# Dummy products from the first cleared columns on, sinks' values off VectorE, a later bias and new orders in a fused attention and MLP-Mixer kernel

## The chip, the cores and the metric

The kernel runs on one core of one Trainium2 chip. The metric is the device time of one launch in microseconds (us), taken as the median of several runs. Beside it stands one profiled execution, with its own time, its span and its trace.

## The reference

Attention with 4 sink keys and a sliding window of 128 runs over 4 batches, 8 heads, 768 positions and 64 dimensions; its output is the input of an MLP-Mixer block (token mixing over positions, then channel mixing). All inputs and the output are float32.

```python
scores = scale * np.matmul(q, k.transpose(0, 1, 3, 2))
keep = is_sink | in_window            # sink: key < 4; window: 0 <= query - key < 128
a = softmax(np.where(keep, scores, -1e9))
x = np.matmul(a, v)                   # 4 x 8 x 768 x 64, then heads side by side: 4 x 768 x 512
h = np.maximum(x.transpose(0, 2, 1) @ w_tok1, 0.0) @ w_tok2     # 768 -> 256 -> 768 over positions
u = x + h.transpose(0, 2, 1)
out = u + np.maximum(u @ w_ch1, 0.0) @ w_ch2                    # 512 -> 1536 -> 512 over channels
```

## The kernel before

The 32 heads are worked on as 16 pairs of heads (pair p = 4 b + n, four pairs a batch b). Work for TensorE is cut into 386 **units** of some tenths of a microsecond. The string `ORDERED` lists them in the order in which TensorE runs them; a letter names the kind, a number the unit, "o1-2" means o1 and o2:

- first batch (pairs 0 to 3): `t` turns q (even numbers) or k (odd numbers) of one pair, 64 columns at a time, into PSUM; `m` writes the additive mask of one group of keys into a score bank (pairs 0 to 2); `s` adds the scores of a group (three groups g = 0 to 2 a pair; s10 is the sinks' scores of pairs 2 and 3); `o0` is the sinks' scores of pairs 0 and 1, `o1` to `o8` are the products with the values, two a pair; `g` and `h` are token mixing of the left and of the right half of the channels (g0, g1, h0, h1 the first product, g2 to g4 and h2 to h4 the second, the rest turnings).
- later batches: `w` turns q and k or u, `a` scores (three units a pair, a0 is pair 4), `n` sinks' scores, `v` products with values (two a pair), `k` token mixing.
- channel mixing of all batches: `c` the first product, `x` and `y` the second. From batch 1 on the first product, and for all batches the second, are done in seven instead of eight block products.

Everything that is not TensorE's work (evictions from PSUM, casts, exponentials, loads, stores) is an `Op` with a cost on each engine that may do it. A planner, run when the kernel is built, keeps a clock for each engine, walks through `ORDERED` and places each pending op on the engine where it ends first by these costs; it thereby fixes the program order on ScalarE (ACT), VectorE (DVE), GpSimd (POOL) and SP. Due times written by hand stand for things the planner can't compute: `landed(7700.0)` is the time at which the sinks' value rows are taken to be in SBUF. A constant `BIAS` of 400 ns is added to VectorE's end time when engines are compared.

Loads of the first batch's q and k (`raws`) are plain float32 transfers issued by SP, and are cast to bf16 by an engine (`cast`; pair 3's by GpSimd or VectorE). All other loads are issued by GpSimd and cast in flight. Their order is `LOADS`: v0 is issued first, then `LOADS` names q, k, v of a pair, `t1`, `t2` the weights of token mixing, `c` and `d` blocks of the weights of channel mixing. At most about seven are outstanding, on eight lanes. From pair 8 on q and k are turned by a transposing DMA that SP issues.

At the start, before any data is there, VectorE clears some tiles, and TensorE multiplies a cleared tile of ones by itself seven times, with 512 columns each, by `keep_warm`. The scores have two double banks of PSUM (`sc`), everything else four single ones.

The code that the diff touches:

Of the kernel before, what the change touches and what calls it, by code (L numbers as in the profile page):

```python
# [17 lines left out]
def kernel(  # L18
# [13 lines left out]
    nc = tc.nc  # L32
    B, H, S, D = q.shape
    P = 128
# [11 lines left out]


    ORDERED = (
# [14 lines left out]
    )  # L63
    LOADS = (
        "q4 v1 k4 t1 v2 t2 v3 q5 k5 c2 q6 v4 k6 c3 c0 c1 k7 q7 v5 d3 d0 d2 k9 v6 k8 v7 d1 q8 v8 q9 k10 q12 v9 "
        "q10 k12 k11 q11 v10 k13 v11 v13 q13 k14 q15 q14 v12 k15 v14 v15 "
    )
    ORDER = (1, 2, 7, 6, 4, 5, 3)
    NQ = 6
# [21 lines left out]
    NSC, NMX = 2, 4  # L91
# [7 lines left out]
    def bank(tag, *shape, dtype=FP32, slot=None):  # L99

        n = given[tag].pop(0) if slot is None else slot
        if tag == "sc":
            return sc[n]
        size = 1
        for x in shape:
            size *= x
        flat = all_banks[:, n]
        flat = (flat if dtype == FP32 else flat.bitcast(dtype))[:, 0:size]
        names = "abc"[:len(shape)]
        return flat.rearrange(  # L110
            f"p ({' '.join(names)}) -> p {' '.join(names)}", **{x: v for x, v in zip(names, shape)},
        )

    in_order = tc.keep_in_program_order
    count = [0]

    def issue(x):
        count[0] += 1
        in_order(x)
# [67 lines left out]
    def mm(*args, **kwargs):  # L187
        issue(nc.tensor.matmul(*args, skip_group_check=True, **kwargs))  # L188
# [4 lines left out]
    def copy(e, out, in_):  # L193
        if e == "ACT":
            in_order(nc.scalar.activation(out, in_, AF.Copy))  # L195
        else:
            in_order({"DVE": nc.vector, "POOL": nc.gpsimd}[e].tensor_copy(out=out, in_=in_))
# [16 lines left out]
    NKB = 3  # L214
    kTb = [singles.tile([P, S], BF16, name=f"kT{n}") for n in range(NKB)]
    ones = kTb[NKB - 1][:, 0:4 * P]
    v_sink_f = t_pool.tile([P, 4, HS * 2], BF16, name="uT_sums").rearrange("p n x -> p (n x)").bitcast(FP32)
    v_sink_f = v_sink_f[:, 0:NHP * 2 * D1].rearrange("p (n i d) -> p n i d", n=NHP, i=2)
    in_order(nc.vector.memset(v_sink_f, 0.0))
    in_order(nc.vector.memset(ones, 1.0))  # L220
    settled = singles.tile([1, 2], BF16)
    in_order(nc.gpsimd.memset(settled, 0.0))
    in_order(nc.scalar.activation(settled[:, 1:2], settled[:, 0:1], AF.Copy))

    def keep_warm(n, slot):
        ps = bank("mx", 4 * P, slot=slot)
        for _ in range(n):
            mm(ps, ones[:, 0:P], ones, start=True, stop=True)

    keep_warm(7, 2 * NSC)  # L230

# [30 lines left out]
    v_sink0 = singles.tile([P, NHP, 2, D1], BF16, name="v_sink")  # L262
# [40 lines left out]
    BLOCK = 1.4  # L303
    RECEIPT = 2100.0
    BIAS = 400.0
    FETCH, FETCH_ALONE = 7200.0, 4600.0


# [16 lines left out]
    def landed(at):  # L325
        op = Op({}, None)
        op.done = at
        return op

    class Plan:  # L330
# [57 lines left out]
        def other(self):  # L388
            best = None
            queue = False  # L390
            for n, op in enumerate(self.pending):

                if op.loads:
                    if queue:
                        continue
                    queue = True
                r = self.ready(op)
                if r is not None and op.loads and len(self.landings) + op.loads > LANES:
                    r = max(r, self.landings[len(self.landings) + op.loads - LANES - 1])
                if r is None:  # L400
                    continue
                at = {
                    e: max([self.free[e], r] + [x[1] for x in op.reads if x[0] != e]) for e in op.cost
                }
                e = min(op.cost, key=lambda e: at[e] + op.cost[e] + BIAS * (e == "DVE"))
                t = at[e]
                if best is None or t < best[0] - 1e-6 or (
                    t < best[0] + 1e-6 and e == best[2] and op.urgent > self.pending[best[1]].urgent
                ):
                    best = (t, n, e)  # L410
            return best
# [1013 lines left out]
        return Op({"POOL": 760.0}, lambda e: fn(), lag=1850.0, loads=1)  # L1425

    plan = Plan()
    plan.free.update(PE=4000.0, ACT=3200.0, DVE=3900.0, POOL=5300.0)
    plan.queue = 12800.0
    plan.landings.append(13500.0)  # L1430

    def queue(key, op):
        done[key] = op
        plan.pending.append(op)
# [9 lines left out]
    def cast(p, n, at):  # L1444
        cost = {"POOL": 765.0, "DVE": 475.0} if p == NHP - 1 else {"DVE": 475.0} if p or n else {"ACT": 750.0}
        return Op(cost, lambda e: copy(e, bf_tile(p, n), raws[p][n]), [landed(at)])

    for p, at in enumerate(((4000.0, 5100.0), (6800.0, 8050.0), (9300.0, 10700.0), (12600.0, 14800.0))):
        for n, name in enumerate(("q_bf", "k_bf")):
            queue((name, p), cast(p, n, at[n]))  # L1450
    v_sink = Op({"POOL": 650.0, "DVE": 345.0, "ACT": 500.0}, lambda e: copy(e, v_sink0, v_sink_f), [landed(7700.0)])
    for n in range(NHP):
        done["vs", n] = v_sink
    plan.pending.append(v_sink)
# [144 lines left out]
```

## Time and profile before

| | |
|---|---|
| median of 3 runs | 192.47 us (192.25 to 193.26) |
| profiled execution, its own time | 191.41 us |
| its span in the trace | 189.7 us |
| matmuls | 2269 |
| TensorE, VectorE, ScalarE, GpSimd busy | 181.5, 160.8, 112.1, 78.5 us |
| HBM read, written | 26.75 MB, 6.29 MB |

In the profile, PE is TensorE's matmuls, PEld its weight loads, DVE VectorE, ACT ScalarE, POOL GpSimd, SP SyncE; SPq and POOLq are issues of DMAs. L188 is line 188 of the kernel, the helper that records every matmul; lines L159, L163 and L191 are turnings. In a timeline a row gives start, length, engine, line, operation, output and input tiles, shapes, and the count of instructions merged into it; in brackets stands the idle time of that engine before it and what ended it. TensorE's lengths overlap, since a product's end is modelled with the time that its last column needs to leave the array.

### The profile page before, as it was taken

To read this page: it belongs to the slowest core of one execution; us is meant where nothing else is said; L and a number is where in the kernel's file an instruction comes from. 1 tells how busy PE (TensorE), PEld (TensorE's weight loads), DVE (VectorE), ACT (ScalarE), POOL (GpSimd) and SP (SyncE) were. 2 spreads that over 40 slices of the span, in tenths; PEclk is the share of its full clock that TensorE was granted. 3 is DMA by queue.
4 is the path that set the end of the run, shared out by engine and by line. 5 is a ranking of instruction groups with operands and counts; after the bars stand their busy time and mean duration, and the time that the engine had idled before them with its cause. 6 is when DMAs were issued, how large, how long until landed. Compare 5 with 4: busy or idle time off the path is not lost.

```text
span 189.7 us, 5560 instructions
## 1 busy us (share of the span) xinstructions
PE 181.5 (96%) x2269; PEld 131.7 (69%) x2269; DVE 160.8 (85%) x343; ACT 112.1 (59%) x210; POOL 78.5 (41%) x122
## 2 busy tenths in 40 slices
PE   5889989999999999999999999999999999999992
PEld 1335758766777888766666788865578887668882
DVE  4766969997699999988999998879998968799882
ACT  4698978999974653858875711488842203773000
POOL 5938566374807989472804970150240000000000
PEclk9999999999999999999999999999999999999999
DMA  5999999999999999999999995431100145200035
GB/s 186 288 276 185 188 193 199 200 197 178 175 141 119 168 117 158 135 149 170 292 119 147 166 117 117 180 146 28 28 5 0 28 86 221 111 0 3 0 138 194
DMA packets 82600, 26.31 MB, mean 139 GB/s; under 512 B 70032, under 2 KB 80272, under 8 KB 82576
## 3 DMA queue, kind: packets, MB, share of 16 engines
q0 software_dynamic: 56864, 11.80, 82.8%
q1 hardware_dynamic: 25088, 13.64, 33.0%
q10 hardware_dynamic: 624, 0.53, 0.8%
q8 instruction: 17, 0.28, 0.6%
q14 instruction: 7, 0.06, 0.2%
HBM read 26.75 MB, written 6.29 MB: 174 GB/s over the span
## 4 chain that ended last, share of the span: by engine, by line
PE 87%; DMA 5%; ACT 2%; DVE 1%; issue 1%; POOL 1%; POOLq 0%
PE ps L188 85%; DMA v_aug<-in_v_dram 5%; ACT pT L692 2%; PE ps L191 1%; PE ps L163 1%; DVE x_sb L781 1%; PE ps L597 1%; ACT kT L195 0%; POOL mask_add L247 0%; POOL mask_add L251 0%; DVE pT L711 0%; DVE o_sb L1276 0%; ACT u_sb L195 0%; DVE recip L778 0%; POOL ident L244 0%
## 5 line engine op out<-in xcount | busy, mean ns | idle before, releaser
L692 ACT ACTIVATE pT<-ps 128x1024 bf16<-128x1024 f32 (+1 forms) x48 | 44.9, 963 | 20.1 <-PE ps L188 19.8
L195 ACT ACTIVATE parts<-ps 128x384 f32<-128x384 f32 x54 | 24.6, 490 | 18.0 <-PE ps L188 16.5
L188 PE MATMUL ps<-uT,w_ch 128*128 128x384 bf16 x168 | 33.7, 326 | 0.0
L1164 DVE CUSTOM_DVE_ANT_0 v1T<-ps,parts 128x384 bf16<-128x384 f32 x54 | 28.1, 552 | 6.4 <-PE ps L188 6.0
L188 PEld LDWEIGHTS <-v1T 128*128 128x128 bf16 x288 | 27.6, 98 | 4.4 <-issue 0.2
L188 PEld LDWEIGHTS <-w_ch 128*128 128x128 bf16 x204 | 19.1, 98 | 10.7
L201 ACT ACTIVATE v1T<-ps 128x384 bf16<-128x384 f32 x41 | 19.8, 497 | 9.4 <-PE ps L188 8.8
L188 PE MATMUL ps<-uT_sums,k_f 128*128 128x384 bf16 x108 | 23.5, 326 | 0.0
L188 PEld LDWEIGHTS <-v_sums 128*128 128x128 bf16 x216 | 20.8, 98 | 3.4 <-issue 0.2
L703 POOL TENSOR_SCALAR_AFFINE_SELECT pT<-pT 128x256 bf16<-128x256 bf16 (+1 forms) x20 | 11.6, 612 | 24.4 <-issue 14.6
L188 PEld LDWEIGHTS <-w_tok 128*128 128x128 bf16 x192 | 18.1, 98 | 4.3 <-issue 1.3
L1276 DVE TENSOR_TENSOR o_sb<-ps,u_sb 128x512 f32<-128x512 f32 (+1 forms) x32 | 17.3, 551 | 3.2 <-PE ps L188 3.2
L188 PEld LDWEIGHTS <-k_f 128*128 128x128 bf16 x144 | 13.6, 98 | 8.3 <-issue 0.6
L188 PE MATMUL ps<-q_f,v1T 128*128 128x256 bf16 x144 | 19.0, 273 | 0.0
L188 PE MATMUL ps<-w_ch,v1T 128*128 128x256 bf16 x144 | 18.8, 273 | 0.0
L188 PE MATMUL ps<-q_f,v_sums 128*128 128x256 bf16 x144 | 18.7, 273 | 0.0
L188 PE MATMUL ps<-v_aug,pT 128*128 128x65 bf16 x352 | 17.7, 194 | 1.0 <-DMA v_aug<-in_v_dram 1.0
L188 PEld LDWEIGHTS <-pT 128*128 128x128 bf16 x352 | 16.2, 98 | 3.0 <-DMA v_aug<-in_v_dram 1.5
L181 POOL DMA_DIRECT2D v_aug<-in_v_dram x16 | 16.5, 1037 | 3.2 <-PE ps L188 1.5
L781 DVE TENSOR_TENSOR x_sb<-ps,recip 128x384 bf16<-128x384 f32 x32 | 17.2, 550 | 0.4
L188 PEld LDWEIGHTS <-kT 64*64 64x64 bf16 (+2 forms) x343 | 7.9, 104 | 13.0 <-issue 9.0
L188 PE MATMUL ps<-qT,kT 64*64 64x192 bf16 (+2 forms) x336 | 15.5, 249 | 0.3 <-ACT pT L692 0.3
(91 smaller groups left out, 301.4 us busy)
## 6 DMA issues: line engine op xcount, KB each, us to landing
v_aug<-in_v_dram POOLq DMA_DIRECT2D x16, 192.0 KB, 10.3
w_ch<-in_moe_w_ch_dram POOLq DMA_DIRECT2D x8, 384.0 KB, 10.9
out_dram<-o_sb SPq DMA_DIRECT2D x6, 512.0 KB, 2.9
out_dram<-o_sb SPq DMA_DIRECT2D x10, 256.0 KB, 2.2
q_f<-in_q_dram SPq DMA_DIRECT2D x4, 384.0 KB, 5.1
k_f<-in_k_dram SPq DMA_DIRECT2D x4, 384.0 KB, 5.8
k_bf<-in_k_dram POOLq DMA_DIRECT2D x16, 96.0 KB, 7.6
q_bf<-in_q_dram POOLq DMA_DIRECT2D x16, 96.0 KB, 10.5
```

The source lines that it names most:

```text
L163: issue(nc.tensor.transpose(outs[x][ds(D * h, D), j], t[rows, h, j], ident[rows, rows]))
L181: in_order(nc.gpsimd.dma_start(out=v_aug.rearrange("p i t d -> p (i t) d")[:, :, 0:D], in_=v[b].rearrange("h s d -> (h s) d")[2 * hp * S:2 ...
L188: issue(nc.tensor.matmul(*args, skip_group_check=True, **kwargs))
L191: issue(nc.tensor.transpose(out, in_, ident))
L195: in_order(nc.scalar.activation(out, in_, AF.Copy))
L201: in_order(nc.scalar.activation(out, in_, AF.Relu))
L597: issue(nc.tensor.transpose(outs[x][columns], rows_by_columns[rows, columns], ident[rows, rows]))
L692: in_order(nc.scalar.activation(part(tiles["pT", p][:, :, ds(2 * g, 2)]), of_keys(tiles["ps_s", p, g])[:, :, 0:width(g)], AF.Exp, scale=scale,
L703: in_order(nc.gpsimd.affine_select(out=pt, in_=pt, compare_op=ALU.is_ge, fill=0.0, base=-n, pattern=[[0, nk], [1 - 2 * n, P]], channel_mul ...
L781: in_order(nc.vector.tensor_tensor(out=x_sb[b][:, ts(half, QH), ts(hp, 2 * D)].rearrange("p t (i d) -> p t i d", i=2), in0=tiles["ps_o", p ...
L1164: in_order(nc.vector._custom_dve(TENSOR_ADD_SAT, out=v1_of(i, half), in0=ps, in1=kept[:, n], s0=HUGE, s1=0.0,))
L1276: in_order(nc.vector.tensor_tensor(out=sb(*out), in0=tiles["ps_out", b, t0, key[0]], in1=in1(), op=ALU.add,))
```

## The change

Four things change.

1. The tile of ones is cleared in two steps: its first 128 columns ahead of the other clearings, the rest behind them. `keep_warm` multiplies twelve times with 128 columns and six times with 512, where it did seven times with 512. The planner's clock for TensorE begins at 4900 ns in place of 4000.
2. The conversion of the sinks' values to bf16 may be placed on GpSimd or ScalarE, no longer on VectorE, and its due time is 8500 ns in place of 7700.
3. `BIAS` counts against VectorE only where its start would be later than 25000 ns (`LEAN_FROM`).
4. `ORDERED` and `LOADS` are other permutations of the same units and loads.

```diff
-        "t0-1 m0-1 s0-1 t2 m2 s2 t3 m3 s3 o0 m4 s4 t4 m5 t5 s5 o1-2 m6 s6 w0 m7 s7 t6 m8 t7 s8 o3-4 s9-10 w1 "
-        "s11-12 g0-1 o5-6 g2 a0 o7-8 a1 g3 w2 a2 h0-1 g4-5 h2-4 n0 a3-4 h5 g6 v0 h6 g7 h7 v1 w3 a5 c5 c3 c0 c8 "
-        "c16 c22 c6 c2 a6-7 w4 c14 c13 v2-3 c1 c19 c23 a8-9 n1 k0 c10 c12 c7 k1-2 a10-11 v4-5 k3 c11 c17 c15 v6 "
-        "c21 c4 c9 v7 x0-1 c20 c18 y0 x2 k4 w5 a12 x6 k5 x3 x7 a13-14 x4 y3 x5 x10 n2 k6 y2 v8 x8 k7 a15 y4 x11 "
...
+        "t0 m0 t1 s0 m1 t2 s1 t3 m2 s2 m3 o0 s3 m4 s4 t4-5 m5 t6 s5 o1-2 m6 s6 w0 m7 t7 s7 m8 o3 s8 o4 s9-10 w1 "
+        "s11-12 g0 o5 g1 a0-1 o6-8 g2-4 w2 a2 h0-1 g5-6 n0 h2-5 a3-4 h6 g7 v0-1 h7 c1 c0 c11 c4 c8 w3 a5 w4 c7 "
+        "v2 c10 c2 c9 v3 n1 a6-7 c6 c13 k0 c20 a8 c3 k1 c12 a9-10 k2 v4-5 c16-17 c14 c5 a11 c15 c19 v6 c21 k3 "
+        "c23 x0 c22 v7 a12-13 x1 c18 w5 x2 x6 k4 x3 y0 k5 x4-5 k6 y3 a14 x7 n2 a15-16 y5 v8 x10 k7 y2 x8-9 x11 "
...
-        "q4 v1 k4 t1 v2 t2 v3 q5 k5 c2 q6 v4 k6 c3 c0 c1 k7 q7 v5 d3 d0 d2 k9 v6 k8 v7 d1 q8 v8 q9 k10 q12 v9 "
-        "q10 k12 k11 q11 v10 k13 v11 v13 q13 k14 q15 q14 v12 k15 v14 v15 "
+        "q4 v1 k4 t1 v2 v3 t2 q5 k5 q6 c2 v4 c0 v5 k6 q7 k7 c3 c1 d3 v6 q8 d2 k8 v7 d0 k9 d1 q9 v10 v8 k12 "
+        "q10 k10 v9 k11 q11 q12 q15 v11 k13 q13 k14 q14 v12 k15 v13 v14 v15 "
...
     ones = kTb[NKB - 1][:, 0:4 * P]
+    in_order(nc.vector.memset(ones[:, 0:P], 1.0))
...
     in_order(nc.vector.memset(v_sink_f, 0.0))
-    in_order(nc.vector.memset(ones, 1.0))
+    in_order(nc.vector.memset(ones[:, P:], 1.0))
...
-    def keep_warm(n, slot):
-        ps = bank("mx", 4 * P, slot=slot)
+    def keep_warm(n, width):
+        ps = bank("mx", width, slot=2 * NSC)
         for _ in range(n):
-            mm(ps, ones[:, 0:P], ones, start=True, stop=True)
-
-    keep_warm(7, 2 * NSC)
+            mm(ps, ones[:, 0:P], ones[:, 0:width], start=True, stop=True)
+
+    keep_warm(12, P)
+    keep_warm(6, 4 * P)
...
+    LEAN_FROM = 25000.0
...
-                e = min(op.cost, key=lambda e: at[e] + op.cost[e] + BIAS * (e == "DVE"))
+                e = min(op.cost, key=lambda e: at[e] + op.cost[e] + BIAS * (e == "DVE" and at[e] > LEAN_FROM))
...
-    plan.free.update(PE=4000.0, ACT=3200.0, DVE=3900.0, POOL=5300.0)
+    plan.free.update(PE=4900.0, ACT=3200.0, DVE=3900.0, POOL=5300.0)
...
-    v_sink = Op({"POOL": 650.0, "DVE": 345.0, "ACT": 500.0}, lambda e: copy(e, v_sink0, v_sink_f), [landed(7700.0)])
+    v_sink = Op({"POOL": 650.0, "ACT": 500.0}, lambda e: copy(e, v_sink0, v_sink_f), [landed(8500.0)])
```

20 rows, old and new, of the table ORDERED are left out of this document.

## The prediction, made before the changed kernel ran

> **What bounds the kernel now.** I read the page's share of busy time first, then the stages, then the chain in order of time, and last the rows of single engines in the first 30 us. The page gives the span, the engines and the chain by engine:
>
> ```profile
> span 189.7 us, 5560 instructions
> PE 181.5 (96%) x2269; PEld 131.7 (69%) x2269; DVE 160.8 (85%) x343; ACT 112.1 (59%) x210; POOL 78.5 (41%) x122
> ...
> PE 87%; DMA 5%; ACT 2%; DVE 1%; issue 1%; POOL 1%; POOLq 0%
> ```
>
> TensorE is the bound, but 96% is a mean over stages. The table by stages, TensorE alone (stage, its length, busy us, matmuls, granted clock, DMA share, GB/s), says where the other 4% lie:
>
> ```profile
> 28.40:60.00 31.60, 31.55 (x466) 1.00 1.72 175
> 60.00:120.00 60.00, 60.00 (x790) 1.00 1.91 154
> 120.00:186.40 66.40, 66.35 (x594) 1.00 0.22 72
> ```
>
> From 28.4 us on TensorE waits 0.1 us in 158. The change leaves the products as they are, and in both orders the array's tiling changes 86 times between units (counted from the two lists), so this part can only stay as it is or get worse. What can be won lies ahead of 28.4. The chain in order of time (start, length, what):
>
> ```profile
> 4.17 10.29 DMA v_aug<-in_v_dram
> ...
> 14.50 1.83 PE ps L188 x32
> ...
> 75.36 111.01 PE ps L188 x1090
> ```
>
> Ahead of 14.50 the end is set by one load, the values of pair 0, issued at 4.17 and landed at 14.46. Between 14.50 and 28.45 the rows of TensorE's timeline (start, length, form, count, idle before) show the waits:
>
> ```profile
> 17.34 0.34 PE L159 MATMUL ps<-ident,q_bf 64*128 64x64 bf16 x12
> 17.61 0.50 PE L188 MATMUL ps<-mask_add,ident 128*128 128x384 bf16 x2
> ...
> 18.23 0.33 PE L188 MATMUL ps<-qT,kT 64*128 64x256 bf16 x4
> 18.49 0.36 PE L188 MATMUL ps<-v_aug,pT 128*128 128x65 bf16 x6
> ...
> 19.50 0.39 PE L188 MATMUL ps<-qT,kT 64*128 64x256 bf16 x4
> 19.82 0.40 PE L188 MATMUL ps<-qT,kTs 64*32 64x512 bf16 x4
> ...
> 20.47 0.39 PE L188 MATMUL ps<-qT,kT 64*128 64x256 bf16 x4
> 21.19 0.34 PE L188 MATMUL ps<-qT,kT 64*128 64x256 bf16 x4 [0.33 <-ACT pT L692]
> 21.46 1.48 PE L188 MATMUL ps<-x_sb,w_tok 128*128 128x256 bf16 x12
> 22.79 0.35 PE L188 MATMUL ps<-v_aug,pT 128*128 128x65 bf16 x6
> ...
> 24.52 0.38 PE L188 MATMUL ps<-qT,kT 64*64 64x256 bf16 x8
> 25.41 0.36 PE L188 MATMUL ps<-v_aug,pT 128*128 128x65 bf16 x6 [0.51 <-DMA v_aug<-in_v_dram]
> ...
> 26.42 0.36 PE L188 MATMUL ps<-qT,kT 64*64 64x192 bf16 x8
> 26.71 0.28 PE L188 MATMUL ps<-x_sb,ident 128*128 128x256 bf16 x1
> ...
> 27.87 0.31 PE L188 MATMUL ps<-qT,kT 64*64 64x192 bf16 x8
> 28.45 1.47 PE L188 MATMUL ps<-x_sb,w_tok 128*128 128x256 bf16 x12 [0.27 <-DVE x_sb L781]
> ```
>
> By the order list these are t6 at 17.34, s8 at 18.23, o3 at 18.49, s9, s10 and s11 from 19.50, s12 at 21.19, g0 and g1 at 21.46, o5 at 22.79, a0 at 24.52, o7 at 25.41, a1 at 26.42, g3 at 26.71, a2 at 27.87, h0 at 28.45. Three waits: s12 for ScalarE to empty a score bank, o7 for the values of pair 3, h0 for VectorE. I price each from start to next start, since the idle column leaves out the modelled tail of the product before. s11 to s12 is 0.72 where s9 to s10 is 0.32: 0.40 lost. a0 to o7 is 0.89 where a1 to g3, as many products, is 0.29: 0.60 lost. a2 to h0 is 0.58 against 0.29: 0.29 lost. Together 1.29 us.
>
> The landings that pace this stretch can be read on GpSimd, which waits for a lane of its load queue (timeline, GpSimd), and from what the queries on v_aug give as least, median and longest time from issue to landing:
>
> ```profile
> 8.74 1.02 POOL L181 DMA_DIRECT2D v_aug<-in_v_dram  x1
> ...
> 13.66 0.82 POOL L197 CAST q_bf<-q_f 128x768 bf16<-128x768 f32 x1 [3.19 <-DMA q_f<-in_q_dram]
> ...
> 18.55 0.75 POOL L206 DMA_DIRECT2D w_ch<-in_moe_w_ch_dram  x1 [0.91 <-DMA v_aug<-in_v_dram]
> ...
> 24.11 0.78 POOL L206 DMA_DIRECT2D w_ch<-in_moe_w_ch_dram  x1 [0.62 <-DMA w_tok<-in_moe_w_tok_dram]
> 25.66 1.48 POOL L206 DMA_DIRECT2D w_ch<-in_moe_w_ch_dram  x2 [0.77 <-DMA v_aug<-in_v_dram]
> ```
>
> ```profile
> DMA to landing us min/median/max: 10.3/10.9/13.5
> ```
>
> GpSimd woke at 25.66 on the load that released TensorE at 25.41, so it sees a landing 0.25 late: v1 was there at 18.30, t2 at 23.86, v3 at 25.41. v2, issued at 8.74, landed by 22.24.
>
> **The change, part by part.** *Dummies.* The rows of the first 11 us:
>
> ```profile
> 2.07 3.17 PE L188 MATMUL ps<-kT 128*128 128x512 bf16 x7 [2.07 <-DVE kT L220]
> ```
>
> ```profile
> 6.16 1.89 PE L188 MATMUL ps<-mask_add,ident 128*128 128x512 bf16 x4
> ...
> 10.82 0.59 PE L188 MATMUL ps<-mask_add,ident 128*128 128x512 bf16 x2 [0.37 <-ACT pT L692]
> ```
>
> The same 512-column product takes 0.43 at first ((1.89 - 0.59)/3, two of the four with the tail) and 0.2 to 0.3 later: the array runs at half rate until after 7 us, although the page's clock digits show nothing of it. Clearing 128 of 512 columns first lets dummies begin at about 1.2 in place of 2.07. Twelve of a quarter width (0.11 each) and six full ones (0.43) take 3.9 at the low rate, to 5.1; the first transposes of before began behind 2.07 + 3.17 = 5.24 less the overlapping tail. So nothing is delayed, and nothing is won before 14.50, because TensorE is there early anyway (0.52 idle for v_aug). One clearing instruction more on VectorE stands ahead of the masks that GpSimd finishes before it issues v0. It can cost 0 to 0.5 (a whole clearing of 512 columns is about that); I take 0.1, and that is on the path.
>
> *Sinks' values.* VectorE loses a conversion of 0.46 at 7.67. On GpSimd it should take between that and the 0.82 of the larger cast at 13.66, beside 3.19 us of idling there; behind it are v2, v3 and t2, queued behind other loads for 10 us and more. On ScalarE it would push exponentials that o1 does not need before 14.50. Nothing on the path, 0 to 0.4 if the waiting for the sinks' rows holds up a cast.
>
> *Leaning to ScalarE from 25 us on only.* More evictions and the casts of pair 3 go to VectorE. The cast of q for pair 3 cannot begin before 13.66 on any engine, and the new order puts t6, which needs it, ahead of s5 and o1. It ends between 14.2 and 14.5, so o1 slips by 0 to 0.4; what slips is taken up by the next wait, at o3.
>
> *Order.* t6 goes ahead of 14.50: 17.61 - 17.34 = 0.27 saved. o3 now precedes s8, so TensorE asks for it at 18.49 - 0.27 - 0.26 = 17.96, but v1 lands at 18.30: 0.34 lost. s8 and o4 follow (o3 and o4 take 1.01, s8 0.26): s9 at 19.57, s12 asked for at 20.86. ScalarE reached s9's exponential at the end of a run of exponentials and evictions; with pair 3's evictions shared out it is earlier by some tenths, so I keep half of the 0.40, 0.20, with 0 and 0.40 as its ends. Then s12 and g0 (0.27 and half of 1.33) to 21.99. The new order asks for v2 here and not after g1, by 22.24: 0.25 lost. g1, a0, a1, o6 follow. In the loads v3 and t2 change places: v3 is there at 23.86, before o7 is reached, and t2 at 25.41, when o8 ends (about 25.4): the 0.60 goes. g2 to g4 and w2 then lie between o8 and h0, so VectorE has 3 us for what h0 needs: the 0.29 goes.
>
> The sum: won 0.27 + 0.40 + 0.60 + 0.29 = 1.56; lost 0.34 + 0.20 + 0.25 + 0.10 = 0.89; net 0.67. The profiled execution's span goes from 189.7 to 189.0, its 191.41 to 190.7; the median of the runs shown, 1.06 above that for reasons the trace does not hold, from 192.47 to **191.8**. Bounds: with the uncertain terms at their good ends 1.1 to 1.4 are won, at their bad ends nothing. What is won is carried to the end only if no new wait comes after 28.4.
>
> **The rivals.** *The landings eat it.* TensorE arriving earlier meets the same first-in-first-out load queue; o3, o5 and g2 are asked for within 0.4 of a landing. For it: 18.30, 22.24 and 25.41 above; against: at 25.41 it has other work in the new order. Then 0.2 remains: 192.3.
>
> *Slower: pair 8's keys are not turned yet.* In the new order a12, the first scores of pair 8, moves ahead of x1; adding up the starts from o5 on puts it at about 58.2, where before it ran here:
>
> ```profile
> 63.59 0.36 PE L188 MATMUL ps<-qT,kT 64*64 64x256 bf16 x8
> ```
>
> Its keys are turned by a DMA from SP, which took long at that place (issues, then the answer on kT for 44 to 62 us):
>
> ```profile
> 48.45 3.79 SPq L555 DMA_TRANSPOSE kT<-k_bf  x2
> ```
>
> ```profile
> DMA to landing us min/median/max: 8.8/8.8/8.8
> ```
>
> Pair 8's is the second of these two, issued at about 51.0 (48.45 + 3.79 less an issue of 1.2) and landed at 59.8. Ahead of k8 the new list has q8 in place of d0 and k9, about one weight block less (near 1.9, between 1.55, the distance of t2 and v3, and twice that for its double size). So the keys are ready at about 57.9 for a request at 58.2. If q8, turned earlier and beside it, slows k8 by a quarter of these 8.8, 2.2, and a second turning holds SP for 0.8 as the first did (2.07 and 1.24 of issue in that answer), TensorE waits 2.7 with everything behind it: 194.5. It decides from keys later than 59.8. Against it: in before nothing waited there.
>
> *The clock.* t0 m0 t1 s0 leaves TensorE idle between t1 and s0 for the time of two evictions. In before it was busy from 2.07 to about 8 before the full rate came; if the pause starts that stretch again at about 7.3, the low rate lasts to 13 and the work of this stage, busy 4.92 in the table by stages, takes twice as long:
>
> ```profile
> 7.97:14.45 6.48, 4.92 (x85) 2.54 (x84) 4.57 (x10) 6.00 (x9) 3.29 (x5) 1.00 1.43 262
> ```
>
> Waits in that stage take up 6.48 - 4.92 = 1.56, so o1 is some 3.0 late, the wait for v1 takes up 0.34, and with ScalarE's overlap half of the rest, 1.3, stays: 193.1. [...]
>
> That the change does not do what it says has no room here, except that the planner may still choose ScalarE for the sinks.
>
> **How the numbers follow.** About 0.5%, 0.96 us, is what a measurement of this kernel can tell from no change: 191.5 and 193.4 are the bounds. The forecast has 0.58, its own range 190.9 to 192.4: half of it below 191.5 (0.29 faster, 0.29 same). The landings have 0.14 (0.02, 0.11, 0.01). Pair 8's keys 0.17, all slower. The clock 0.11 (0.01, 0.04, 0.06). Together 0.32, 0.44, 0.24. The range of 190.7 to 193.7 leaves out about 0.05 below, and above 0.11 of the keys and 0.02 of the clock.
>
> **What would show it.** Right: o7 and h0 without a wait; o3 and o5 idle for v_aug by 0.2 to 0.4; h0 at about 27.8 with g4 done; no idle time of TensorE after 28 us. Wrong: an idle TensorE ahead of a12 or w4 with a DMA as releaser; products of the masks of pair 1 still at 0.43 after 10 us; v0 landing later than 14.7; the span's stages after 60 us longer for the same products.

## The result, and the profile after

The changed kernel takes 193.11 us (median of 20 runs, 191.72 to 194.39); the kernel before, run beside it, takes 191.95 (20 runs, 191.0 to 193.26). The ratio is 1.0059, with an interval of 1.0036 to 1.0083: slower by about 1.1 us, where 0.7 less was forecast. The comparisons leave disturbed runs out.

The profiled execution took 192.94 us; its page, the head, the chain by engine, and the instruction queue:

```profile
span 191.1 us, 5605 instructions
PE 182.1 (95%) x2280; PEld 133.0 (70%) x2280; DVE 162.6 (85%) x350; ACT 112.8 (59%) x212; POOL 73.8 (39%) x114
...
q8 instruction: 18, 0.29, 0.7%
...
PE 72%; DMA 19%; DVE 3%; ACT 2%; POOL 1%; issue 1%; SPq 0%; POOLq 0%
```

The span is 1.4 longer. The chain of what ended last is less TensorE (72% for 87%) and more DMA (19% for 5%): new waits stand on it. TensorE's stages, as shown of before (stage, its length, busy us, matmuls, granted clock, DMA share, GB/s):

```profile
28.10:60.00 31.90, 31.80 (x483) 1.00 1.76 175
60.00:76.00 16.00, 15.20 (x212) 1.00 2.42 143
76.00:186.60 110.60, 110.60 (x1165) 1.00 0.94 104
```

From 60 to 76 us TensorE idles 0.8; before, it idled 0.1 in all of 28.4 to 186.4. The timeline of TensorE in the first 29 us (start, length, form, count, idle before):

```profile
5.08 0.50 PE L159 MATMUL ps<-ident,q_bf 64*128 64x64 bf16 x12
...
14.61 0.35 PE L159 MATMUL ps<-ident,q_bf 64*128 64x64 bf16 x12 [0.91 <-POOL q_bf L197]
...
15.05 0.36 PE L188 MATMUL ps<-v_aug,pT 128*128 128x65 bf16 x6
...
18.50 0.35 PE L188 MATMUL ps<-v_aug,pT 128*128 128x65 bf16 x6
...
20.84 0.39 PE L188 MATMUL ps<-qT,kT 64*128 64x256 bf16 x4
21.45 0.34 PE L188 MATMUL ps<-qT,kT 64*128 64x256 bf16 x4 [0.21 <-ACT pT L695]
...
22.39 0.35 PE L188 MATMUL ps<-v_aug,pT 128*128 128x65 bf16 x6
...
25.43 0.27 PE L188 MATMUL ps<-x_sb,ident 128*128 128x256 bf16 x1
...
25.76 0.27 PE L188 MATMUL ps<-x_sb,ident 128*128 128x256 bf16 x1
...
28.13 1.05 PE L188 MATMUL ps<-x_sb,w_tok 128*128 128x256 bf16 x8
```

By the order list these are t0, t6 at 14.61, o1 at 15.05, o3 at 18.50, s11, s12, o5 at 22.39, g2 at 25.43 and 25.76, h0 at 28.13. Last, the end of the chain (start, length, what), and the stores in the stretch from 181 us on (issues, KB each, median us to landing):

```profile
76.47 110.17 PE ps L188 x1092
186.64 0.02 issue
186.66 0.42 DVE o_sb L1279
```

```profile
q8 instruction: 1, 0.02, 1.2%
...
out_dram<-o_sb SPq DMA_DIRECT2D x3, 256.0 KB, 3.8
out_dram<-o_sb ACTq DMA_DIRECT2D x4, 128.0 KB, 3.7
```

Of the kernel before, the instruction queue on its page (in the stretch from 181 us it has no packet), the last eviction, and the stores in that stretch:

```profile
q8 instruction: 17, 0.28, 0.6%
```

```profile
186.39 0.42 DVE o_sb L1276
```

```profile
out_dram<-o_sb SPq DMA_DIRECT2D x4, 256.0 KB, 2.1
out_dram<-o_sb ACTq DMA_DIRECT2D x4, 128.0 KB, 2.1
```

So the last eviction begins 0.27 later (186.66 for 186.39), and from there to the end of the span it takes 4.4 for 3.3. Of the 1.4 us, 0.3 lie ahead of the last eviction and 1.1 behind it, where the change touches nothing. The table splits the spans by units (starts from the timelines by the order lists; y27 is the last unit; the tail runs from the start of the last product to the end of the span):

| profiled execution | o1 at | o1 to h0 | h0 to y27 | tail | span |
|---|---|---|---|---|---|
| before | 14.50 | 13.95 | 157.09 | 3.62 | 189.7 |
| after | 15.05 | 13.07 | 157.68 | 4.72 | 191.1 |

t6 (0.27) and g4 (0.66, the distance of g4 and g5 before, 29.75 to 30.41; a unit of this kind has two products with the identity, each with two of token mixing behind it, so the rows at 25.43 and 25.76 are both g2's) changed sides: for the same work, o1 to h0 took 14.34 before (13.95 - 0.27 + 0.66) and h0 to y27 156.43. In the changed kernel, then, o1 is 0.55 later, 0.27 of it t6 itself; o1 to h0 is 1.27 shorter, h0 to y27 1.25 longer, the tail 1.10 longer: 0.28 - 1.27 + 1.25 + 1.10 = 1.36. (From y27 to the last product it is 0.55 and 0.54.)

### The profile page after: what moved, and what is told of

The parts are those of the page before. It is cut to its first block, busy times and chain, and to the rows that moved or that the text cites. A ratio compares the mean times of both kernels' runs of the same rounds, so it can differ in the third digit from the quotient of the medians.

```text
span 191.1 us, 5605 instructions
## 1 busy us (share of the span) xinstructions
PE 182.1 (95%) x2280; PEld 133.0 (70%) x2280; DVE 162.6 (85%) x350; ACT 112.8 (59%) x212; POOL 73.8 (39%) x114
## 4 chain that ended last, share of the span: by engine, by line
PE 72%; DMA 19%; DVE 3%; ACT 2%; POOL 1%; issue 1%; SPq 0%; POOLq 0%
PE ps L188 70%; DMA w_ch<-in_moe_w_ch_dram 7%; DMA v_aug<-in_v_dram 6%; DMA q_f<-in_q_dram 4%; DMA k_f<-in_k_dram 2%; ACT pT L695 1%; POOL k_bf L173 1%; DVE o_sb L1279 1%; PE ps L191 1%; DVE u_sb L934 1%; DVE qT L197 1%; PE ps L600 1%; DVE x_sb L784 1%; POOL q_bf L197 0%; SPq L136 0%
## 5 line engine op out<-in xcount | busy, mean ns | idle before, releaser
L188 PE MATMUL ps<-uT,w_ch 128*128 128x384 bf16 x168 | 34.6, 326 | 0.0
L1167 DVE CUSTOM_DVE_ANT_0 v1T<-ps,parts 128x384 bf16<-128x384 f32 x54 | 28.7, 553 | 4.0 <-PE ps L188 3.4
L188 PEld LDWEIGHTS <-v1T 128*128 128x128 bf16 x288 | 27.8, 98 | 4.7 <-issue 0.4
L188 PE MATMUL ps<-w_ch,v1T 128*128 128x256 bf16 x144 | 18.2, 273 | 0.1
L188 PEld LDWEIGHTS <-kT 64*64 64x64 bf16 (+2 forms) x354 | 9.2, 106 | 10.6 <-issue 8.4
L173 POOL DMA_DIRECT2D k_bf<-in_k_dram x16 | 13.4, 844 | 5.8 <-DMA k_bf<-in_k_dram 2.6
```

Source lines behind the costliest of these rows:

```text
L173: in_order(nc.gpsimd.dma_start(out=out[:, h], in_=rows[:, h]))
L1167: in_order(nc.vector._custom_dve(TENSOR_ADD_SAT, out=v1_of(i, half), in0=ps, in1=kept[:, n], s0=HUGE, s1=0.0,))
```

## The experiments

Four theories stand in the expectations. A: 22 TensorE instructions more (11 products, each with a weight load) bring an 18th packet of instructions into the last stores. B: the order of the last units, with the waits at 59 to 71 us, carries the whole loss. C: the pauses of the new start make the clock fall back. D: weight block d1, now loaded behind the keys of pair 9, comes late. Each experiment was timed beside the kernel before. Its ratio is to those runs; it is estimated over all compared runs and need not be the quotient of two medians. Start and length of an instruction packet are those of the queue's records in the trace.

**e1_seven.** The changed kernel with seven dummies:

```diff
-    keep_warm(12, P)
+    keep_warm(1, P)
     keep_warm(6, 4 * P)
```

> The changed kernel with seven dummy products (one of 128 columns, six of 512) in place of eighteen; the planner is told the old count, so every engine's order stays. Theory A, instruction fetch: eleven products fewer are 22 TensorE instructions fewer, the 18th packet of the instruction queue is gone, the span ends 3.3 us after the last product's issue as before the change and not 4.4; time 1.1 us lower, ratio to before about 1.000 (0.998 to 1.002). Theory B, the order of the last units and the waits at 59 to 71 us carry the whole loss: nothing changes, ratio 1.006 and the end still 4.4 us behind the last product.

192.3 us, ratio 1.0024 [0.999, 1.0059]. Its profiled execution had a granted clock of 0.982 and the packet all the same, at 186.5, with a tail of 4.57. Theory A had no packet there, so by this profile alone it would fall; e1_again repeats it at full clock.

**e2_before_11more.** The kernel before, and ahead of the first real unit:

```diff
+    [mm(..., ones[:, 0:32], ones[:, 0:32], ...) for _ in range(11)]
```

> The kernel before with eleven dummy products of 32 columns more behind its seven, hidden ahead of the first values; everything else in its order. Theory A: an 18th instruction packet appears within the last 8 us and the end behind the last product grows from 3.3 to about 4.4 us; ratio 1.004 to 1.007. Theory B: eleven hidden products cost nothing, ratio 1.000 (0.998 to 1.002).

192.13 us, ratio 1.0009 [0.9978, 1.0041]. The packet came, at 183.2 and 1.1 long (after: 183.9 and 1.9 long), and the tail grew from 3.62 to 4.22. The last unit began 0.5 sooner in this execution, so the span stayed at 189.8. The mechanism shows; the loss that theory A expected (1.004 to 1.007) does not.

**e3_after_30more.** The changed kernel with 30 more such products of 32 columns.

> The changed kernel with thirty dummy products of 32 columns more still, hidden ahead of the first values. Theory A: the 18th instruction packet is asked for thirty products, some 3 us, earlier (at about 181 and not 183.9) and is gone before the last stores; the end shrinks to 3.3 us, ratio about 1.000 (0.998 to 1.003) although TensorE has thirty products more. Theory B: no effect or a loss, ratio 1.006 to 1.010.

193.5 us, ratio 1.0088 [1.0051, 1.0126]. The tail is 3.60, although there are most instructions here: the packet came at 182.9, 51 products ahead of the end in place of 23, and was through before the last stores. So it is the packet's place, not the number of packets, that lengthens the tail. The ratio is above what A allowed (0.998 to 1.003), so something else costs. Its timeline of TensorE has three waits that the changed kernel's does not: two for which the trace names nothing ("issue"), and one for a late turning of q:

```profile
30.30 0.70 PE L188 MATMUL ps<-x_sb,w_tok 128*128 128x256 bf16 x5 [0.49 <-issue]
...
44.54 0.39 PE L188 MATMUL ps<-qT,kTs 64*32 64x512 bf16 x3 [0.52 <-issue]
...
88.06 0.39 PE L188 MATMUL ps<-qT,kTs 64*32 64x512 bf16 x2 [0.72 <-DMA qT<-q_bf]
```

**e4_before_orders.** The kernel before with the new `ORDERED` and `LOADS`, nothing else.

> The kernel before with the two new lists alone (its own dummies, bias and sinks' conversion). Theory A and the landing of the weight block d1: 17 packets, the end 3.3 us; in the middle the early gain of 0.7 to 1.0 us is given back by waits at 59 to 71 us of about 1.2 us; ratio 1.000 to 1.003. Theory B: the lists carry the loss, ratio 1.005 to 1.008.

191.86 us, ratio 1.001 [0.9982, 1.0038]. Tail 3.59, no 18th packet. From h0 to y27 it takes 157.57, in the changed kernel 157.68, so the longer stretch comes with the lists; the lists as they stand are not shown to win or lose. The last units in their new order end as before, and the ratio is below what theory B asked for (1.005 to 1.008): the lists are not the whole loss.

**after_again.** The changed kernel unaltered, beside the next three.

> The changed kernel once more, unaltered, beside the others of this call. Theory A (the last instruction packet): a packet of the instruction queue in the last 8 us and the end 4.2 to 4.7 us behind the last product's issue; theory C (the clock): about 9 of 20 runs at a granted clock of 0.991 or less, as before; ratio about 1.006. If the packet is there and the end is 3.6 us, A falls.

192.8 us, ratio 1.0022 [0.9984, 1.006], where about 1.006 was expected; the tail 4.77, with a packet at 184.2. The clock fell back in this profile (below).

**e5_orders_d1.** e4 with one change of the loads:

```diff
-v7 d0 k9 d1 q9
+v7 d0 d1 k9 q9
```

> The kernel before with the two new lists, and in the loads d1 ahead of k9. Theory D (the late weight block d1 holds VectorE and through it TensorE at 59 to 71 us): d1 lands by about 54 and not 59.2 us, the waits of x1, x2, y3 and a15, about 1.2 us in sum, go; ratio 0.994 to 0.997. Rival: the waits only move (to a15 by k9's turning, or to n3), ratio 1.000 to 1.002.

191.18 us, ratio 0.9962 [0.9925, 0.9999]. d1 landed at 54.88, where it was 59.66 in e4, 59.23 in the changed kernel and 54.29 before. The stretch from 60 to 76 us has no idle time left:

```profile
60.00:76.00 16.00, 16.00 (x263) 1.00 2.24 147
```

**e6_orders_d1_t6** and **e6_again.** e5 with t6 behind the first products with values, run twice:

```diff
-m5 t6 s5 o1-2 m6
+m5 s5 o1-2 t6 m6
```

> As the last, with s5 and o1-2 ahead of t6 again. If the cast of pair 3's q holds up o1 (15.05 us where its values are there at 13.8), o1 begins at 13.9 to 14.5 and 0.3 to 0.8 us more are won, ratio 0.990 to 0.995; if the landings of v1, v2 and t2 set the pace up to 25 us all the same, ratio as in the last run.

> The kernel before with the new lists, d1 ahead of k9 and t6 behind o2, once more, unaltered. 0.9949 [0.9913, 0.9985] was measured. A gain that is one of the lists comes out at 0.993 to 0.998 again; 0.999 or above would say that the first result was partly chance.

191.1 us, ratio 0.9949 [0.9913, 0.9985], and 191.01, 0.9961 [0.9926, 0.9995]. It is faster than both kernels. What the second edit adds to e5 is too little for these intervals.

**e7_after_oldstart.** The changed kernel with the first 13 units in their old order.

```diff
-t0 m0 t1 s0 m1 t2 s1 t3 m2 s2 m3 o0 s3 m4
+t0-1 m0-1 s0-1 t2 m2 s2 t3 m3 s3 o0 m4
```

> The changed kernel with the first units in the old order (t0-1 m0-1 s0-1 t2 m2 s2 t3 m3 s3 o0), the rest as changed. Theory C: the pauses of TensorE behind t1 and behind m1, together with the early dummies, make the clock gate fall back to half rate for 3 to 7 us in nearly half of the runs; without them at most 1 of 12 runs is at 0.991 or less, time 0.25 to 0.5 us lower than the changed kernel, ratio 1.002 to 1.004. Rival: the lower clock is not due to these pauses, 4 to 6 of 12 runs stay at 0.991 or less and the ratio at 1.006.

193.17 us, ratio 1.0062 [1.0027, 1.0096], above the 1.002 to 1.004 of theory C: the pauses are not what makes the changed kernel slower. The granted clock of the whole run was 0.992 or less in 2 of 12 runs, against 13 of 32 of the changed kernel.

**e8_orders_11more.** e4 with the eleven products of e2.

> The kernel before with the new ORDERED and LOADS and 11 dummy products of 32 columns more; the dummies' time on the array is small, the count of TensorE's instructions is that of the changed kernel (4574). If the 18th packet of TensorE's instructions at the end makes most of the loss (tail of 4.7 in place of 3.6 us in the changed kernel), the packet shows at about 183 to 184, the last product's issue is followed by 4.2 to 4.8 us, and the ratio to before is 1.004 to 1.007, against 1.001 for the lists alone. If the count is nothing, the tail is 3.6 and the ratio 1.000 to 1.002.

192.72 us, ratio 1.0043 [1.0005, 1.0082]. The packet came at 184.6 and the tail is 4.24, as theory A had it. But the last unit is later too, 186.51 for 185.77 in e4, with more waiting between 58 and 71 us (0.36 for pair 8's keys and 0.60 for d1, in e4 0.19 and 0.20), so not all of the 0.0033 between the ratios of e8 and e4 is the tail.

**e9_after_d1_t6.** The changed kernel with the two edits of e6.

> The changed kernel with weight block d1 loaded ahead of k9 and t6 behind o2 (the two edits that took the kernel with the new lists from 1.001 to 0.995). If the late block and the tail are the two causes, the middle's waits (1.4 us between 58.6 and 70.6) go, last products start near 184.5 in place of 185.8, the tail stays at 4.7 or more, and the ratio is 0.998 to 1.001. If the dummies, the bias and the sinks' conversion cost something else, it stays at 1.004 or above; if nothing but the lists matters it is 0.995.

191.9 us, ratio 0.9989 [0.9956, 1.0022], inside what the two causes gave. Its stages and its last eviction:

```profile
28.80:60.00 31.20, 31.20 (x478) 1.00 1.72 175
60.00:76.00 16.00, 16.00 (x262) 1.00 2.07 154
76.00:186.00 110.00, 109.99 (x1109) 1.00 0.81 104
```

```profile
186.02 0.42 DVE o_sb L1279
```

The middle is clean, the last eviction is 0.37 earlier than before's, and yet the span is 190.5 for 189.7: the packet is there at 183.4 and the tail is 4.78.

**e1_again.** e1_seven unaltered.

> The changed kernel with 7 dummies in place of 18 (one of 128 columns, six of 512), once more, because its profiled execution stood at a lower clock than the others. If the count of instructions decides where the 18th packet falls, a profile at full clock has no packet in the last 8 us, a tail of 3.6 us, and a time near before's (ratio 1.000 to 1.002). If it is chance from execution to execution, the packet is there at 184 to 187 with a tail of 4.5 us or more, and the ratio 1.002 to 1.006.

192.35 us, ratio 1.0021 [0.9989, 1.0054], a little above what A alone allowed. At full clock no packet is in the stretch from 181 us to the end of the span; the only one left came at 191.6, behind it. The stores are back:

```profile
out_dram<-o_sb SPq DMA_DIRECT2D x3, 256.0 KB, 2.2
out_dram<-o_sb ACTq DMA_DIRECT2D x4, 128.0 KB, 2.1
```

```profile
186.42 0.42 DVE o_sb L1279
```

The last eviction is 0.24 earlier than in the changed kernel, and the span 1.4 shorter (189.7).

Profiles side by side, in the columns of the first table (before and e2 have g4 behind h0 and t6 behind o1; e6, e6_again and e9 have t6 behind o1):

| profiled execution | o1 at | o1 to h0 | h0 to y27 | tail | 18th packet, products left |
|---|---|---|---|---|---|
| before | 14.50 | 13.95 | 157.09 | 3.62 | none |
| e2 | 13.86 | 14.05 | 157.09 | 4.22 | 183.2, 22 |
| after | 15.05 | 13.07 | 157.68 | 4.72 | 183.9, 23 |
| after_again | 16.30 | 13.05 | 156.43 | 4.77 | 184.2, 20 |
| e3 | 15.80 | 13.07 | 159.01 | 3.60 | 182.9, 51 |
| e7 | 14.98 | 13.08 | 158.01 | 4.66 | 184.2, 23 |
| e8 | 15.29 | 13.07 | 158.15 | 4.24 | 184.6, 23 |
| e9 | 15.35 | 13.46 | 156.36 | 4.78 | 183.4, 21 |
| e4 | 15.14 | 13.05 | 157.57 | 3.59 | none |
| e5 | 15.49 | 13.06 | 156.36 | 3.59 | none |
| e6 | 14.32 | 13.72 | 156.36 | 5.28 | 186.5, 0 |
| e6_again | 16.18 | 13.46 | 156.36 | 3.60 | none |
| e1_seven | 17.33 | 13.05 | 156.73 | 4.57 | 186.5, 11 |
| e1_again | 15.38 | 13.05 | 157.14 | 3.61 | 191.6, 0 |

The 17th packets come with 128 to 143 products left (128 to 134 in before, e1 and e4 to e6, with seven dummies; 142 or 143 in the changed kernel, e2, e7, e8 and e9). By the page of the changed kernel 18 packets carry 2280 products with their weight loads, about 253 instructions or 127 products each; from one packet to the next 143 - 23 = 120 products were counted, near it. With seven dummies the 18th is due a few products ahead of the end (128 to 134 less 120 to 127), and its place varies: at 11 in e1_seven, behind the last product in e6 and e1_again, not within the profile in the others; with eleven products more it is due some 20 products ahead of the end in every profile (20 to 23), just when the last stores go out.

**The late block.** What it stops is seen in the changed kernel. The chain from 44 us on:

```profile
44.93 1.68 POOL k_bf L173 x2
46.61 12.62 DMA w_ch<-in_moe_w_ch_dram
59.23 0.04 issue
59.27 1.47 PE ps L188 x10
...
67.65 0.41 DVE o_sb L1279
68.06 0.67 DVE v_sums L1233
68.73 0.60 DVE u_sb L934
```

GpSimd issues the keys of pair 9 (line 173), then d1 at 46.61; d1 lands 12.62 later, and TensorE's x1 starts on it at 59.27. VectorE, in program order, waits for the same block (its timeline), and what queues behind it reaches TensorE up to eleven microseconds later:

```profile
59.25 1.03 DVE L1487 TENSOR_TENSOR q_f<-w_ch 128x768 bf16<-128x768 bf16 x2 [1.78 <-DMA w_ch<-in_moe_w_ch_dram]
```

```profile
58.63 0.55 PE L188 MATMUL ps<-qT,kT 64*64 64x256 bf16 x16
...
68.11 0.81 PE L188 MATMUL ps<-q_f,v_sums 128*128 128x256 bf16 x6 [0.50 <-DVE o_sb L1279]
...
70.58 0.54 PE L188 MATMUL ps<-qT,kT 64*64 64x256 bf16 x16 [0.30 <-DVE u_sb L934]
```

Before, d1 landed at 54.29 and VectorE took it up at 55.27 without waiting:

```profile
55.27 1.02 DVE L1484 TENSOR_TENSOR q_f<-w_ch 128x768 bf16<-128x768 bf16 x2
```

**The clock.** A table of stages cut at the recorded changes of the rate, and between them every 3.41 us: so long is the stretch at half rate in after_again (11.19 to 14.60), and in the changed kernel and in the one before the full rate is recorded for 184.32 and 180.91 us (5.53 to 189.85 and 8.09 to 189.00), 54 and 53 times 3.413. First after_again, then the first such stretch of e1_seven, e9, e1_again and the changed kernel:

```profile
4.36:7.77 3.41, 2.41 (x33) 1.00 0.93 249
7.78:11.19 3.41, 1.61 (x35) 1.00 1.36 284
11.19:14.60 3.41, 3.41 (x16) 0.50 1.37 277
14.60:18.01 3.41, 3.26 (x77) 1.00 1.71 182
```

```profile
5.55:8.96 3.41, 1.65 (x20) 1.00 1.09 280
```

```profile
5.93:9.34 3.41, 1.82 (x34) 1.00 1.15 261
```

```profile
5.47:8.88 3.41, 1.97 (x34) 1.00 1.14 296
```

```profile
5.53:8.94 3.41, 2.33 (x39) 1.00 1.23 292
```

After 1.61, 1.65 and 1.82 busy of 3.41 us the rate halved; after 1.97 and 2.33 it did not. Busy time alone does not decide it, though: among the last products the full rate outlasted a stretch with 1.49 busy (e1_seven, 186.45 to 189.87) and one with 1.65 (e6_again, 185.17 to 188.58), and was lost after 1.32 (after_again, 185.27 to 188.68). What else counts is open. In after_again one stretch at half rate, itself fully busy, brought the full rate back, and o1 came 1.25 later than in the other profile of the same kernel; in e1_seven it took two, the first 2.58 busy.

A full rate that comes late is not seen in a run's granted clock. In e6_again its first record stands at 14.51; until then two products of 512 columns take 1.03 or 1.04, as in after_again's stretch at half rate (1.01 and 1.04) and not 0.6 as later. Its o1 is at 16.18, and its clock reads 1.000.

## Why the prediction was wrong, point by point

**The first 28 us: the gain came, by other terms than forecast.** Predicted was a net gain of 0.67. Measured are 0.32 at h0 (28.45 to 28.13) and 0.66 of g4, which now lies ahead of it: 0.98. (The sign "h0 at about 27.8 with g4 done" leaves g4's own 0.66 out; with it the sum puts h0 at 28.4.) By terms:

- o7 and h0 wait no more, as forecast (0.60 and 0.29). From start to next start a0 and a1 took 1.18 before and take 0.48 now, a2 0.58 and 0.24: 0.70 and 0.34 won. s11 to s12 is 0.61 for 0.32, so 0.29 of waiting is left where 0.20 was taken.
- o3 and o5 were to lose 0.34 and 0.25 to v1 and v2. They wait for neither (no brackets at 18.50 and 22.39): v1 and v2 landed at 16.89 and 20.97 by the queue's records, 1.4 and 1.3 earlier than before. The landings of before were taken as fixed; the time from issue to landing is not. It differs between executions of one kernel too (v0 lands at 13.79 and 14.95 in the two profiles of the changed kernel). The rival of the landings fails: in e8, with v1 at 18.23 and v2 at 22.36 as before, o3 and o5 do not wait either, since TensorE comes later, behind an o1 at 15.29.
- t6 was to be a gain of 0.27, with a slip of 0 to 0.4 at o1 that o3's wait would take up. q of pair 3 was cast on GpSimd from 13.73 to 14.55, t6 began at 14.61 and o1 at 15.05, 0.55 late, and no wait at o3 took it up. So the gain of 0.27 became a loss of 0.28. The unit that was moved ahead waited for its own input and held up o1, whose values had landed at 13.79.
- A cost of the clearing is not seen: v0 was issued at 4.18, before at 4.17. Nor of the sinks' values: GpSimd converted them in 0.82, the upper bound; v2 was issued 0.80 later for it and landed earlier all the same, and the next cast began at 13.73, where it was 13.66 before.

Better than forecast were o3 and o5 (0.59), the clearing (0.10), a0 to a2 (0.15) and some 0.1 of small differences; worse were t6 (0.55) and s12 (0.09). That the gain came out within 0.3 of the sum is luck, since the misses run both ways.

**"Nothing is delayed" by the dummies.** True of the array: t0 began at 5.08, about where the old dummies ended (2.07 + 3.17 = 5.24 less the overlapping tail). (The 0.43 of a product at half rate holds, the first four masks start 0.40 to 0.43 apart; but the 0.59 subtracted for it is the length of two products at the full rate, near that of one at half (0.63, the last dummy of before at 4.61) by chance.) It failed at the other end of the kernel. The dummies were costed as time on TensorE and not as 22 instructions, and the step that moved 1.10 us was not in the sum at all. That a packet due some 20 products before the end goes with stores that take 3.0 to 4.0 us in place of 2.1 or 2.2 is shown by after, after_again, e1_seven, e7, e8, e9 and e2 on one side and before, e4, e5, e6_again, e1_again and e3 on the other; e8 and e4 differ in the eleven products alone. e6 has a long tail (5.28), with its packet behind the last product and without late stores by the median, and is left unexplained.

On the times the effect is smaller: the ratios of kernels with the packet exceed those of their partners without it by 0.0018 (the mean of the two results of the changed kernel over the mean of the two of e1), 0.0033 (e8 over e4), 0.0034 (e9 over the mean of the two of e6, which lack the new bias, the sinks' conversion and the early dummies as well) and 0.0009 (e2 over no change), about 0.45 us in the mean, and no pair's intervals separate. The two series of the changed kernel together (32 runs, mean 192.98) and the two of e1 (23 runs, 192.23) differ in the eleven dummies alone, and clearly: by 0.75 with a 95% interval of 0.36 to either side, their spans by 0.98 (0.35). So the eleven products cost time. They may cost less than 1.10 because a kernel with seven dummies has the packet in some executions too (e1_seven), or behind the span: outside it, five of 12 runs of e1_again take 2.3 to 2.8 us, the changed kernel at most 2.0. No run shows which. Nor does any take out `BIAS` or the sinks' conversion alone; e1 has both and stands 0.0011 to 0.0014 above e4, within the intervals.

**"Carried to the end only if no new wait comes after 28.4."** This step named its own condition, and the condition failed: 1.25 us between h0 and y27. The slower rival looked at the right place, but in this profile at the wrong victim. Its keys of pair 8 came in time, a12 starting at 58.63 without a wait (forecast 58.2); in e4 and e8 a12 did wait for them, 0.19 and 0.36. What was late was the load behind the next pair's keys: k9's two halves took 3.4 and 2.9 us to land behind one another while pair 8's keys were being turned, and d1, which the new list puts directly behind them, landed 4.9 us later than before. (That the turning slowed k9 is read from the times alone; no run took the turning away. In before too the loads of that stretch were slow, two halves of a q that landed at 57.41 and 59.03, 3.1 and 1.6 behind the ones ahead; d1 had landed before them.) The prediction followed the loads that had moved ahead (q8) and not d1, which stands behind them. Shown by e5, e6 and e9: with d1 ahead of k9 the stretch is 156.36 in all four profiles, as long as the 156.43 of before for the same work, and the ratio falls by 0.005 to 0.006 from e4 to e5 and e6, and by 0.005 from the changed kernel (1.0040, the mean of two) to e9. That "this part can only stay as it is or get worse" held: it got worse, by the waits, and without them it stayed.

**The clock.** What the rival feared exists: the rate falls back in the new start, in 13 of 32 runs judged by a clock of 0.992 or less. The pause of the forecast, between t1 and s0, is one of three: TensorE waits 0.58 there, and 0.50 and 0.20 ahead of t2 and t3 for VectorE's casts. That the pauses alone let the rate fall is not shown (2 of 12 runs in e7, without them; none in e2 and e3; e4, e5 and e6, with the same pauses behind the dummies of before, had 1 of 35 and e6_again 2 of 12; e1 10 of 24, e8 4 of 12; what share the dummies have in it stays open, and the count misses a rate that rises late, as in e6_again). But it was priced at 1.3 us, and those 13 runs are only 0.5 longer than the others of the same kernel (193.42 for 192.87, 193.10 for 192.56). after and after_again show why: o1 is 1.25 later in the second, and the last evictions begin at 186.66 and 186.63. From h0 to y27 after_again takes 156.43, as before: it reaches d1 so late that it hardly waits for it (0.01 us in its chain from 22.67 to 186.61). The late block takes up what the clock loses; in these two the costs are not added. In e9, without the late block, the difference is 0.64 (192.11 for 191.47, 6 of 12 runs).

How long a low rate lasts, the rival had estimated at 5.7 us (7.3 to 13), with o1 3.0 late. Recorded are 3.41 in after_again (11.19 to 14.60) and 6.83 in e1_seven (8.96 to 15.79), with o1 1.25 and 1.95 later than in the other profile of the same kernel.

**The base.** The forecast of 191.8 was 0.67 below a median of 192.47 from three runs; 20 runs gave 191.95, and the result is 1.16 above that; over both series the changed kernel's mean is 1.00 above that of the kernel before, with an interval of 0.32 to either side. As an estimate, the 0.67 that was to be won, the 0.005 of the late block (0.96) and the 0.75 of the eleven products make 1.04.

## What to carry to other kernels

Follow a reordered load list to the blocks that land later, not only to those that moved ahead, and to every engine that takes them in program order: one weight block behind two slow loads cost more (1.25 in the profile) than was won at the start (0.98). Look up where the packets of instructions fall, above all at the end of the kernel: eleven products, 22 of TensorE's 4560 instructions, cost 0.75 us between two series though they run ahead of the first values, and in the profiles with them the 18th packet came among the last stores (tails of 4.72 and 4.77; without them 3.61 and 4.57). And a stretch that waits for a landing can take up what was lost or won ahead of it (here 1.25 at o1 between two profiles, 0.03 at the last eviction), so remove the latest such wait first; with d1 ahead of k9 the same lists gave 0.9962, and with t6 moved back as well 0.9949 and 0.9961.

## What the runs showed of the hardware that was not expected

- In seven profiles with a packet of TensorE's instructions (16 KB, 1.1 to 1.9 us long) among the last stores, these take 3.0 to 4.0 us in the median in place of 2.1 or 2.2, and the tail is 4.2 to 4.8 in place of 3.6.
- The clock halved after stretches of 3.41 us with 1.61, 1.65 and 1.82 us of products in them, at the start, and stayed after 1.49 and 1.65 at the end: TensorE was idle in none of them throughout, and busy time alone does not tell.
- In e3, with thirty short products more at the start, TensorE idles 0.49 and 0.52 us at 30 and 44 us for no reason that the trace names.
